# Halved first transfers, ScalarE diagonals and a re-ordered prologue in an attention and MLP kernel

## The chip, the cores and the metric

One core of a Trainium2 chip. The metric is device time in microseconds (us) of the whole program, the median of several runs. TensorE (PE, with its weight loads as PEld), VectorE (DVE), ScalarE (ACT) and GpSimd (POOL) each work through a list of instructions in order and wait for each other by semaphores; SyncE (SP) issues the transfers (DMAs) between the chip's main memory and SBUF.

## The reference, cut to what matters

```python
# r, k, v: (4, 8, 768, 48);  w, u: (8, 48)
for t in range(S):                       # S = 768
    cur = einsum('bhd,bhe->bhde', u * kt, vt)
    y[:, :, t] = einsum('bhd,bhde->bhe', rt, state + cur)
    state = w * state + einsum('bhd,bhe->bhde', kt, vt)
x = y.transpose(0, 2, 1, 3).reshape(B * S, H * D)      # 3072 x 384
h = x @ w_in                                          # 384 x 2048
g = 0.5 * h * (1 + erf(h / sqrt(2)))
out = g @ w_out                                       # 2048 x 384
```

## The kernel before, in words

The recurrence is done in chunks of 128 time steps (six chunks), each in four groups of two heads. For a group of the first chunk `first_group` (L525) does this: DVE multiplies keys and receptances `T` by powers of w into `Ts` (L535) and multiplies keys with receptances into `RK` (L541); PE sums `RK` with weights `u` (`sum_pairs`, L549); ACT copies the eight sums per row from PSUM to `cs` (L554); POOL spreads them over the diagonal of `Am` with one select over 128 x 1024 elements (`on_diagonal`, L496); PE makes the scores from `Ts` (L562); DVE copies their lower triangle over `Am` (L567, a predicated copy); PE multiplies `Am` by the values (L581); `keep` splits the result into a high and a low part, ACT for the high one (L509), DVE for the low one (L510). The score products of a group use the same PSUM bank as its sums, so they wait for the copy to `cs`.

The powers of w come first: a small transfer brings w and u (`wu_sb`, L357), DVE clamps w into `W` (L407), squares up to 64 powers (L412) and makes the inverses (L418, L419); ACT makes further powers (`state_powers`, L430 and L428) and copies them into `E` (L451).

The MLP runs in 96 steps: six chunks, 16 slices of 128 hidden units. A step has nine products for the first layer (`moe1`, L768), two Gelus on ACT (L800, L801), a difference on DVE (L802), and nine products for the second layer (`moe2`, L812). In the first 16 steps the weights of each slice must be split into two parts: a transfer of 768 KB (L464), three ACT operations (L479, L482, L488) and two DVE operations (L484, L491). Groups of later chunks (`prepare`, `products`, `state`) are put between the steps. PE is kept warm before the first step by products of zeros (L395) wherever the plan has a gap. At the end of a chunk the three banks `O` are scaled and stored; the last chunk's third bank is cut in two halves (`O[2]` and `Y`), each scaled by ACT (L851) or DVE (L848) and stored by SP (L854).

`count_plain` (L872) counts how many w lie in the range for which this form holds: DVE (L867 to L871), a product (L875), a copy to an integer (L877), and a load of it into a register of every engine (`values_load`, L878). After the last step all engines branch on it (L989).

The order on every engine is made by the class `Plan`: each operation is given an engine, a duration, a due time and the names it reads and writes; `play` simulates the engines and issues in order of simulated start, and a random search over due times with a fixed seed keeps the order whose simulated end is earliest. A change of any entry can therefore change the order everywhere. `port=True` marks operations of DVE and POOL that the plan doesn't let overlap; a POOL operation so marked gets a real wait on the last such DVE operation before it.

Of the kernel before, what the change touches and what calls it, by code (L numbers as in the profile page):

```python
# [24 lines left out]
C = 128  # L25
# [25 lines left out]
AT_LOADS, AT_E = 14000, 15000  # L51

SCALE = ("dd", "d", "d", "d")
PRODUCT = ("d", "d", "d", "d")

# [219 lines left out]
def rwkv_gelu_mlp(tc, rkT, rkv, wuT, uN, wmlp, r, k, vT, w, u, out):  # L275
    nc = tc.nc
    with ExitStack() as ctx:
# [63 lines left out]
        pool = lambda n: 200 + n * 2.1  # L341
        select_ns = lambda n: 100 + n * 8 * 1.5

# [26 lines left out]
        add("pool", 290, 4, lambda: select(ident, 0, -1, ALU.is_equal), r=["ones"], w=["ident"])  # L370

        for x in wa:
            add("pool", 750, 5, lambda x=x: nc.gpsimd.memset(x, 0), w=["wa"], port=False)

# [29 lines left out]

        def powers():
            nc.vector.memset(W[:, :, HALF:HALF + 1], 1.0)
            nc.vector.tensor_scalar(out=W[:, :, HALF + 1:HALF + 2], in0=w_sb.unsqueeze(2), scalar1=WMIN, scalar2=WMAX,  # L407
                                    op0=ALU.max, op1=ALU.min)
            n = 1
# [11 lines left out]

        add("dve", 1500, 5, powers, r=["w_sb"], w=["P"], port=True)
        add("dve", 520, 6, inverses, r=["P"], w=["Wi"], port=True)

# [17 lines left out]

        add("act", 1700, LATER, state_powers, r=["P"], w=["WKs"])
# [4 lines left out]
        add("pool", 320, 5, lambda: nc.gpsimd.memset(E[32:64, :, :, 1], 1.0), w=["E0"], port=False)  # L448
        for i, (src, dst, h) in enumerate(((slice(0, LP), slice(0, LP), 0), (slice(0, D), slice(64, LP), 1),
                                           (slice(64, LP), slice(0, D), 1))):  # L450
            add("act", act(512), AT_E, lambda src=src, dst=dst, h=h: nc.scalar.copy(  # L451
                out=E[dst].rearrange("l p a h i -> l (p a) h i")[:, :, h],
                in_=W[src].rearrange("l p (a i) -> l (p a) i", a=2)[:, :, 32:32 + HALF]),
                r=["Wi", "P", "WKs"], w=[f"E{(1, 2, 0)[i]}"], port=False)
# [66 lines left out]
        def first_group(gi, at, XX, XB, y, YB):  # L521
# [6 lines left out]
            sums, CS = cs[gi], f"cs{gi}"  # L528
            halves = SCALE[gi]
            for i, e in enumerate(halves):  # L530
                nb = NB // len(halves)
# [5 lines left out]
                        in1=W[:, p, 0:C].unsqueeze(1).unsqueeze(1).to_broadcast([LP, 2, nb, C]), op=ALU.mult),  # L537
                    r=["P", "Wi", f"T{gi}"], w=[f"{TR}{b}" for b in range(bs.start, bs.stop)], port=True)
            me = PRODUCT[gi]
            mul = nc.vector.tensor_tensor if me == "d" else nc.gpsimd.tensor_tensor  # L540
            add("dve" if me == "d" else "pool", dve(512) if me == "d" else pool(512), LATER, lambda: mul(  # L541
                out=RK[gi], in0=T[gi][:LP, 0, :, ::-1], in1=T[gi][:LP, 1], op=ALU.mult), r=[f"T{gi}"], w=[f"RK{gi}"], port=True)

            def sum_pairs():
                for b in range(NB):
                    for h in range(2):
# [268 lines left out]
        def moe2(m, at, dest):  # L815
# [3 lines left out]

            def go(m, n, which, at):  # L820
                j = m % NJ
                high, low, GH, GL = hidden(m)
                add("pe", MM * sum(parts[i][3] - parts[i][2] for i in which) / TOK, at, lambda: [product2(j, high, low, n, parts[i]) for i in which],
                    r=[f"{('wh', 'wl', 'wh')[n]}{2 * j + 1}", (GH, GH, GL)[n]], w=[banks[i] for i in which])

# [8 lines left out]
            elif m == NSTEP - 1:  # L834
                for q, i in ((1, 0), (1, 1), (5, 2), (4, 2), (0, 0), (0, 1), *((q, 2) for q in range(LEFT - 3, -1, -1)),
                             *((q, 3) for q in range(LEFT - 1, -1, -1))):
                    at += 2000
                    for n in range(3):
                        go(m - q, n, (i,), at + n)
            if j < NJ - 1:  # L840
                return
            last = m == NSTEP - 1
            for i, (d, bank, a, b) in enumerate(parts):
# [9 lines left out]
                if last:  # L853
                    dma(512 * (b - a), at + 2000, lambda d=d, a=a, b=b, o=o: nc.sync.dma_start(dest[d][:, a:b], o), r=[R])  # L854
            if not last:
                dma(128 * 6144, at + 20000, lambda: nc.sync.dma_start(
                    dest.rearrange("d p n -> p d n"), flat2(raw[0]).bitcast(F32).rearrange("p (d n) -> p d n", d=3)),
                    w=[f"raw0{i}" for i in range(3)])

# [12 lines left out]

        def count_plain(at):
# [76 lines left out]
        def swap():  # L950
# [7 lines left out]
        add("do", 0, SWAP_DUE, swap, w=["late", "ident", "ones", "diag", "past", "P", "WKs", "WN", "zeros", "warm", "spread"] +  # L958
            ["Wi"] + [f"{x}{i}" for x in ("T", "RK", "Nk", "Nv") for i in range(NP)] +
            [f"Ts{i}{b}" for i in range(NP) for b in range(NB)] + [f"Am{i}{j}" for i in (2, 3) for j in range(2)])  # L960
# [4 lines left out]
        for G in range(NSTEP + 1):  # L965
# [114 lines left out]
```

## Time and profile before

| | us |
|---|---|
| median of 3 runs (lowest, highest) | 449.92 (449.80, 450.51) |
| the profiled execution's own time | 449.15 |
| its span, first to last instruction | 447.0 |
| PE busy | 438.1 (98%) |
| DVE, ACT, POOL busy | 228.7, 178.7, 81.2 |
| granted TensorE clock, mean | 0.998 |

PE matmuls are pipelined and their ends modelled, so 98% is not PE at its peak; what matters is whether the next product could start. The profiled execution lies 2.15 us above its span and 0.77 us under the median of the runs.

### The profile page before, as it was taken

The numbers are of one execution on the slowest core, as the hardware profiler recorded it, in microseconds if no ns is written. First come the engines' busy times: TensorE is split into PE (matmuls) and PEld (weight loads), VectorE is DVE, ScalarE is ACT, GpSimd is POOL, SyncE is SP. The second block draws the span as 40 slices with busy tenths as digits, with TensorE's granted clock in tenths as the row PEclk, the third lists the DMA queues.
The fourth block names the chain that finished last, engine by engine and source line by source line (L and its number), as shares of the span: only waits on it lengthen the run. The fifth ranks groups of instructions, "written<-read, shape, count | busy, mean of one in ns | idle before, by whom it ended". The sixth has DMA issues, their size and how long they took to land.

```text
span 447.0 us, 10460 instructions
## 1 busy us (share of the span) xinstructions
PE 438.1 (98%) x4618; PEld 378.2 (85%) x4618; DVE 228.7 (51%) x342; ACT 178.7 (40%) x305; POOL 81.2 (18%) x98
## 2 busy tenths in 40 slices
PE   7999999999999999999999999999999999999995
PEld 5788888888888887888888888888888888888884
DVE  7989999975624367153546343544434311211111
ACT  7699998432322223232224222223322223322221
POOL 5533130324110222011211202202202000000000
PEclk9999999999999999999999999999999999999999
DMA  7986785223303034030333121313403000100002
GB/s 299 409 295 251 263 300 191 87 79 120 114 2 113 1 114 172 0 114 4 110 112 118 57 72 41 114 32 108 145 3 111 13 1 13 71 1 0 1 1 76
DMA packets 13570, 46.15 MB, mean 103 GB/s; under 512 B 1808, under 2 KB 2192, under 8 KB 13520
## 3 DMA queue, kind: packets, MB, share of 16 engines
q1 hardware_dynamic: 13520, 45.42, 29.7%
q8 instruction: 38, 0.62, 0.6%
q14 instruction: 12, 0.10, 0.1%
HBM read 38.73 MB, written 4.72 MB: 97 GB/s over the span
## 4 chain that ended last, share of the span: by engine, by line
PE 96%; DVE 1%; ACT 1%; DMA 0%; issue 0%; POOL 0%; DVEq 0%
PE Hp L768 42%; PE O L812 41%; PE Y L678 3%; PE A L686 2%; PE Y L706 2%; PE A L695 2%; PE Y L812 1%; PE O L581 1%; PE A L562 1%; PE O L768 1%; PE Y L562 0%; PE O L575 0%; ACT W L428 0%; PE A L603 0%; DMA wu_sb<-in_wuT_dram 0%; DVE W L412 0%
## 5 line engine op out<-in xcount | busy, mean ns | idle before, releaser
L768 PE MATMUL Hp<-xx,wh 128*128 128x512 f32 x570 | 156.3, 382 | 0.0
L800 ACT ACTIVATE gh<-Hp 128x512 fp32r<-128x512 f32 x91 | 54.3, 597 | 187.7 <-PE Hp L768 187.7
L802 DVE TENSOR_TENSOR gl<-gf,gh 128x512 fp32r<-128x512 f32 x92 | 65.7, 714 | 117.7 <-ACT gf L801 115.1
L768 PEld LDWEIGHTS Hp<-xx,wh 128*128 128x128 f32 x570 | 105.6, 189 | 15.4 <-issue 0.2
L768 PE MATMUL Hp<-xx,wl 128*128 128x512 f32 x285 | 77.4, 379 | 0.0
L812 PE MATMUL O<-gl,wh 128*128 128x512 f32 (+1 forms) x276 | 74.3, 376 | 0.8 <-DVE Sa L735 0.8
L812 PE MATMUL O<-gh,wl 128*128 128x512 f32 (+1 forms) x276 | 74.0, 375 | 0.0
L812 PE MATMUL O<-gh,wh 128*128 128x512 f32 (+1 forms) x276 | 73.9, 375 | 0.0
L768 PEld LDWEIGHTS Hp<-xx,wl 128*128 128x128 f32 x285 | 53.7, 189 | 7.7
L812 PEld LDWEIGHTS O<-gh,wh 128*128 128x128 f32 x276 | 52.0, 189 | 7.7 <-ACT gh L800 0.4
L801 ACT ACTIVATE gf<-Hp 128x512 f32<-128x512 f32 x95 | 56.3, 593 | 5.3 <-PE Hp L768 4.1
L812 PEld LDWEIGHTS O<-gl,wh 128*128 128x128 f32 x276 | 51.0, 189 | 8.3 <-issue 1.2
L812 PEld LDWEIGHTS O<-gh,wl 128*128 128x128 f32 x276 | 51.3, 189 | 6.8
L634 DVE TENSOR_TENSOR Tb<-Tb,E 112x1024 f32<-112x1024 f32 x20 | 26.5, 1325 | 31.4 <-DMA Tb<-in_rkT_dram 31.3
L637 POOL TENSOR_TENSOR Nb<-Nb 128x384 f32<-128x384 f32 x20 | 20.3, 1017 | 112.0 <-DMA Nb<-in_rkv_dram 48.8
L640 POOL TENSOR_TENSOR Nb<-Nb,WN 128x384 f32<-128x384 f32 x20 | 26.3, 1316 | 32.4 <-DVE Tb L634 19.4
L646 DVE TENSOR_REDUCE cs<-Nb 128x8 f32<-128x384 f32 x20 | 11.0, 552 | 24.1 <-POOL Nb L643 24.1
L735 DVE SCALAR_TENSOR_TENSOR Sb<-Sa,E,A 48x192 f32<-48x192 f32 x40 | 16.5, 413 | 11.2 <-PE A L695 10.5
L643 POOL TENSOR_TENSOR Nb<-Nb,u_sb 128x384 f32<-128x384 f32 x20 | 20.1, 1003 | 9.6 <-DVE gl L802 9.6
L509 ACT CAST xx<-Y 112x512 fp32r<-112x512 f32 x15 | 8.8, 585 | 31.7 <-PE Y L706 31.7
L716 POOL MEMSET done<- 1x1 f32 x19 | 1.7, 89 | 105.2 <-PE Y L678 105.2
L479 ACT ACTIVATE wa<-raw 128x768 f16<-128x768 bf16 x16 | 19.4, 1209 | 0.0
(128 smaller groups left out, 384.5 us busy)
## 6 DMA issues: line engine op xcount, KB each, us to landing
raw<-in_wmlp_dram SPq DMA_DIRECT2D x16, 767.8 KB, 5.6
Nb<-in_rkv_dram SPq DMA_DIRECT2D x20, 576.0 KB, 4.5
Tb<-in_rkT_dram SPq DMA_DIRECT2D x20, 512.0 KB, 6.0
out_dram<-raw SPq DMA_DIRECT2D x5, 768.0 KB, 3.7
T<-in_rkT_dram SPq DMA_DIRECT2D x4, 512.0 KB, 5.2
xx<-x SPq DMA_DIRECT2D x30, 64.0 KB, 4.4
N<-in_rkv_dram SPq DMA_DIRECT2D x4, 384.0 KB, 10.0
out_dram<-raw SPq DMA_DIRECT2D x2, 256.0 KB, 4.1
```

Of the source, the lines that this page charges most:

```text
L479: add("act", 930 if j < 2 else 1110, LATER, lambda: nc.scalar.activation(out=a.bitcast(F16).rearrange("p (n t) -> p n t", t=2)[:, :, 1], i ...
L634: add("dve", 1140, LATER, lambda: nc.vector.tensor_tensor(out=flat, in0=flat, in1=E[:, p, 0].rearrange("l h i -> l (h i)").unsqueeze(1).to ...
L637: add("pool", pool(DM), LATER, lambda: nc.gpsimd.tensor_tensor(out=n[:, 0], in0=n[:, 0], in1=n[:, 1], op=ALU.mult), r=[NK], w=[NR])
L640: add("pool", pool(DM), LATER, lambda: nc.gpsimd.tensor_tensor(out=kn, in0=kn, in1=WN2[:, p].rearrange("s j d -> s (j d)").unsqueeze(1).to ...
L643: add("pool", pool(DM), LATER, lambda: nc.gpsimd.tensor_tensor(out=n[:, 0], in0=n[:, 0], in1=u_sb[:, p, :].unsqueeze(1).to_broadcast([C, N ...
L678: last[:] = [nc.tensor.matmul(YU[quarter(j), h, b * HALF:(b + 1) * HALF], lhsT=S2[h][l, b, :], rhs=t[l, 0, b, times(h)], start=(b == 0), s ...
L735: add("dve", 430, at, lambda l=l, x=x: nc.vector.scalar_tensor_tensor(out=out[quarter(1 - x)], in0=src[l], scalar=E[l, p, 1, h, 32:33], in ...
L768: nc.tensor.matmul(dst, lhsT=wt[j][:, 0, k_ * 128:(k_ + 1) * 128], rhs=pairs(x[:, a, k_, :]), start=start and k_ == ks[0], stop=stop and k ...
L800: add("act", 480, LATER, lambda: nc.scalar.activation(out=high, in_=dst, func=AF.Gelu, scale=256.0), r=[H_], w=[GH])
L801: add("act", 480, LATER, lambda: nc.scalar.activation(out=gf, in_=dst, func=AF.Gelu, scale=256.0), r=[H_], w=["gf"])
L802: add("dve", dve(512), LATER, lambda: nc.vector.tensor_tensor(out=low, in0=gf, in1=high.bitcast(F32), op=ALU.subtract), r=["gf", GH], w=[G ...
L812: nc.tensor.matmul(dst[:, a:b], lhsT=wt[j][:, 1, d * 128:(d + 1) * 128], rhs=pairs(gt)[:, a // 2:b // 2], start=(j == 0 and n == 0), stop= ...
```

## The change

1. `T[0]` comes in two transfers (batches 0 and 1, then 2 and 3); the product `RK[0]` and its sums on PE are done by the same halves. Other groups keep one transfer, one product, one set of sums.
2. The diagonals of groups 0 and 2 are no longer made by a POOL select but by eight ACT operations of 128 x 128 each (a copy of `diag` scaled by one column of the sums). Groups 1 and 3 keep the select, now with `port=True`, and with 1.08 us in the plan where it had 1.64 us.
3. The clamp of w is an operation of its own, due before all else on DVE. The second `memset` of `wa` on POOL and the `memset` of `E` now wait for it; the first doesn't.
4. Durations in the plan: inverses 520 to 560 ns, state powers 1700 to 2080, copies to `E` 487 to 630, the `memset` of `E` 320 to 520.
5. `count_plain` moves from step 32 to step 38, its DVE part now behind that step's low Gelu part, and the register load is an entry of 620 ns on DVE instead of 0 ns on no engine.
6. In the last steps the products into `Y` (the fourth part) are ordered behind those into `O[2]`.
7. The store of the third piece of the last chunk is issued by ACT instead of SP. The stores of the five other chunks are each cut in two transfers (two thirds and one third).

```diff
-            dma(C * 4096, at, lambda: nc.sync.dma_start(T[s], rkT[gi]), r=r, w=[f"T{s}"])
+            for bs in (slice(0, 2), slice(2, 4)) if gi == 0 else (slice(0, NB),):
+                dma(C * 1024 * (bs.stop - bs.start), at, lambda bs=bs: nc.sync.dma_start(
+                    T[s][:, :, bs], rkT[gi][:, :, bs]), r=r, w=...)
...
+        add("dve", 170, -10 ** 6, clamp, r=["w_sb"], w=["P0"], port=True)
+        for n, x in enumerate(wa):
+            add("pool", 750, 5, lambda x=x: nc.gpsimd.memset(x, 0), r=["P0"] * n, w=["wa"], port=False)
+        add("dve", 1380, 5, powers, r=["P0"], w=["P"], port=True)
...
-            add("pe", 650, LATER, sum_pairs, r=[f"RK{gi}", "w_sb"], w=XB)
+            for bs in parts:
+                nb = bs.stop - bs.start
+                add("dve", dve(128 * nb), LATER, lambda bs=bs: nc.vector.tensor_tensor(
+                    out=RK[gi][:, bs], in0=T[gi][:LP, 0, bs, ::-1], in1=T[gi][:LP, 1, bs], op=ALU.mult),
+                    r=TN(bs), w=[f"RK{gi}{bs.start}"], port=True)
+                add("pe", 220 + 110 * nb, LATER, lambda bs=bs: sum_pairs(bs), r=[f"RK{gi}{bs.start}", "w_sb"], w=XB)
...
-            add("pool", select_ns(C), LATER, lambda: on_diagonal(am, C, sums), r=[CS], w=[f"{AM}0", f"{AM}1"], port=False)
+            if OWN[gi] == "s":                                   # OWN = "asas"
+                add("pool", select_ns(C), LATER, lambda: on_diagonal(am, C, sums), r=[CS], w=[f"{AM}0", f"{AM}1"], port=True)
+            else:
+                for n in range(2 * NB):
+                    j, b = divmod(n, NB)
+                    add("act", 185 + C / 1.2, LATER, lambda n=n, j=j, b=b: nc.scalar.activation(
+                        out=am[:, j, b, :], in_=diag, func=AF.Copy, scale=sums[:, n:n + 1]), r=["diag", CS], w=[f"{AM}{j}"])
...
+                if last and i == 2:
+                    add("act", 400, at + 1000 + i, lambda d=d, a=a, b=b, o=o: nc.scalar.dma_start(dest[d][:, a:b], o), r=[R])
...
-            add("dve", 800, at, in_range, r=["w_sb", "xx00h"], w=["n1"])
+            add("dve", 800, at, in_range, r=["w_sb", behind], w=["n1"])
...
-            add("do", 0, at, lambda: plain.append(nc.values_load(n2, min_val=0, max_val=LP * NP)), r=["n2"])
+            add("dve", 620, at, lambda: plain.append(nc.values_load(n2, min_val=0, max_val=LP * NP)), r=["n2"])
...
-            if G == 2 * NJ:
-                count_plain(step_at(G))
+            if G == 2 * NJ + 6:
+                count_plain(step_at(G), hidden(G)[3])
```

## Rows read from the trace of the kernel before

**Rows 1.** Busy time by stage (stretch: length, busy us of each engine, clock, DMA)

```profile
5.25:15.39 10.14, 8.82 (x174) 6.65 (x175) 9.15 (x13) 7.43 (x19) 4.39 (x3) 1.00 1.01 399
15.39:22.76 7.37, 7.37 (x134) 5.54 (x134) 7.37 (x8) 5.40 (x8) 4.82 (x4) 1.00 1.02 397
34.00:50.00 16.00, 16.00 (x194) 13.77 (x193) 15.79 (x23) 16.00 (x20) 3.08 (x4) 1.00 0.75 266
85.00:441.90 356.90, 355.93 (x3551) 310.28 (x3541) 148.59 (x232) 105.80 (x194) 51.63 (x63) 1.00 0.20 65
```

**Rows 2.** Chain of work that ended last: one undisturbed run of nine products

```profile
45.07 1.94 PE Hp L768 x9
```

**Rows 3.** Timeline of PE, then DVE, around the count at 169 us (start, us, instruction)

```profile
168.68 0.81 PE L812 MATMUL O<-gh,wh 128*128 128x512 f32 x3
169.55 0.09 PEld L875 LDWEIGHTS A<-n 112*1 112x1 f32 x2 [0.47 <-DVE Sb L735]
...
170.66 0.15 DVE L877 CAST n<-A 1x1 int32<-1x1 f32 x1
...
171.35 0.51 PEld L812 LDWEIGHTS O<-gl,wh 128*128 128x128 f32 x3 [1.17 <-issue]
...
172.11 0.81 PE L768 MATMUL Hp<-xx,wh 128*128 128x512 f32 x3
```

**Rows 4.** Tile n: the register load (ns min/median/max, first and last start)

```profile
L878 PEldq TENSOR_LOAD <-n x1: 485/485/485, 170.8 to 170.8; - x1
```

**Rows 5.** Line 854's instructions, then the timeline of the last stores

```profile
L854 SPq DMA_DIRECT2D out_dram<-raw x3: 343/382/2007, 439.8 to 440.7; - x3
...
439.78 2.92 SPq L854 DMA_DIRECT2D out_dram<-raw  x3
439.93 0.39 ACT L851 ACTIVATE raw<-O 128x256 f32<-128x256 f32 x1 [0.17 <-PE O L812]
441.94 0.42 DVE L848 TENSOR_SCALAR Nb<-Y 128x256 f32<-128x256 f32 x1 [1.87 <-PE Y L812]
442.80 0.37 SPq L854 DMA_DIRECT2D out_dram<-Nb  x1
```

**Rows 6.** The clamp and its neighbours at the start, and line 867, its like

```profile
2.43 0.79 DVE L407 TENSOR_SCALAR W<-wu_sb 112x4 f32<-112x4 f32 x1 [0.91 <-DMA wu_sb<-in_wuT_dram]
2.46 0.74 POOL L373 MEMSET wa<- 128x768 int32 x1
...
L867 DVE TENSOR_SCALAR low<-wu_sb x1: 159/159/159, 116.1 to 116.1; 112x4 f32<-112x4 f32 x1
```

**Rows 7.** Timeline of DVE and POOL around the first diagonals

```profile
5.25 0.69 DVE L541 TENSOR_TENSOR RK<-T 112x512 f32<-112x512 f32 x1
8.41 3.18 POOL L496 TENSOR_SCALAR_AFFINE_SELECT Am<-cs 128x1024 f32<-128x1024 f32 x2 [4.63 <-ACT cs L554]
10.46 1.30 DVE L567 COPY_PREDICATED Am<-past,A 128x1024 f32<-128x1024 uint32 x1 [0.99 <-POOL Am L496]
```

**Rows 8.** Timeline of ACT: what stands after each of its idle times

```profile
12.92 0.17 ACT L554 COPY cs<-A 128x8 f32<-128x8 f32 x1 [2.49 <-PE A L549]
12.98 1.09 ACT L479 ACTIVATE wa<-raw 128x768 f16<-128x768 bf16 x1
16.07 0.17 ACT L554 COPY cs<-Y 128x8 f32<-128x8 f32 x1 [0.76 <-PE Y L549]
20.48 0.59 ACT L509 CAST xx<-O 128x512 fp32r<-128x512 f32 x1 [1.30 <-PE O L581]
25.23 0.48 ACT L607 COPY Sa<-A 112x384 f32<-112x384 f32 x1 [1.03 <-PE A L603]
```

**Rows 9.** ACT line 428 by shape, 0 to 40 us (us busy, mean ns), then its merged timeline row

```profile
L428 ACT ACTIVATE W<-W 112x64 f32<-112x64 f32 x4 | 1.1, 335 | 0.0
L428 ACT ACTIVATE W<-W 112x32 f32<-112x32 f32 x4 | 0.9, 304 | 0.0
...
4.90 1.91 ACT L428 ACTIVATE W<-W 112x64 f32<-112x64 f32 x8
```

**Rows 10.** Transfers issued at 1.29 and at 3.87 us (count, KB, us to landing)

```profile
T<-in_rkT_dram SPq DMA_DIRECT2D x1, 512.0 KB, 3.4
...
raw<-in_wmlp_dram SPq DMA_DIRECT2D x1, 767.8 KB, 8.6
```

**Rows 11.** Timeline, DVE and PE: the weights of the fifth slice and their first use

```profile
39.03 1.69 DVE L491 TENSOR_TENSOR wl<-wb,wh 128x768 fp32r<-128x768 f32 x1
40.90 0.81 PE L768 MATMUL Hp<-xx,wl 128*128 128x512 f32 x3
```

More of the change, by code (lines that the diff above doesn't have):

```diff
@@ L51 @@
 AT_LOADS, AT_E = 14000, 15000
+OWN = "asas"
 SCALE = ("dd", "d", "d", "d")
-PRODUCT = ("d", "d", "d", "d")
 class Plan:
@@ L350, in load_group @@
             s = slot(gi)
-            dma(C * 4096, at, lambda: nc.sync.dma_start(T[s], rkT[gi]), r=r, w=[f"T{s}"])
+            for bs in (slice(0, 2), slice(2, 4)) if gi == 0 else (slice(0, NB),):
+                dma(C * 1024 * (bs.stop - bs.start), at, lambda bs=bs: nc.sync.dma_start(
+                    T[s][:, :, bs], rkT[gi][:, :, bs]), r=r, w=[f"T{s}{b}" for b in range(bs.start, bs.stop)] if gi == 0 else [f"T{s}"])
             if gi < NP:
@@ L370, in rwkv_gelu_mlp @@
         add("pool", 290, 4, lambda: select(ident, 0, -1, ALU.is_equal), r=["ones"], w=["ident"])
-        for x in wa:
-            add("pool", 750, 5, lambda x=x: nc.gpsimd.memset(x, 0), w=["wa"], port=False)
         for dst, src, x in ((diag2, diag, "diag"), (past2, past, "past")):
@@ L402, in rwkv_gelu_mlp, with clamp @@
         plan.heat_from = add("pe", 430 * HEATS, 10, warm_up, r=["zeros"], w=["H", "A0", "A1", "O0", "O1", "O2", "Y", "U"])
-        def powers():
+        def clamp():
             nc.vector.memset(W[:, :, HALF:HALF + 1], 1.0)
@@ L408, in powers @@
                                     op0=ALU.max, op1=ALU.min)
+        def powers():
             n = 1
@@ L420, in inverses @@
                                            op=ALU.mult)
-        add("dve", 1500, 5, powers, r=["w_sb"], w=["P"], port=True)
-        add("dve", 520, 6, inverses, r=["P"], w=["Wi"], port=True)
+        add("dve", 170, -10 ** 6, clamp, r=["w_sb"], w=["P0"], port=True)
+        for n, x in enumerate(wa):
+            add("pool", 750, 5, lambda x=x: nc.gpsimd.memset(x, 0), r=["P0"] * n, w=["wa"], port=False)
+        add("dve", 1380, 5, powers, r=["P0"], w=["P"], port=True)
+        add("dve", 560, 6, inverses, r=["P"], w=["Wi"], port=True)
         def state_powers():
@@ L529, in first_group @@
             halves = SCALE[gi]
+            parts = (slice(0, 2), slice(2, 4)) if gi == 0 else (slice(0, NB),)
+            TN = lambda bs: [f"T{gi}{b}" for b in range(bs.start, bs.stop)] if gi == 0 else [f"T{gi}"]
             for i, e in enumerate(halves):
@@ L537, in first_group, with sum_pairs @@
                         in1=W[:, p, 0:C].unsqueeze(1).unsqueeze(1).to_broadcast([LP, 2, nb, C]), op=ALU.mult),
[L538 to L545, printed above, removed]
+                    r=["P", "Wi", *TN(bs)], w=[f"{TR}{b}" for b in range(bs.start, bs.stop)], port=True)
+            def sum_pairs(bs):
+                for b in range(NB)[bs]:
                     for h in range(2):
@@ L818, in moe2, with go @@
             banks = ["O0", "O1", "O2", "Y"][:len(parts)]
-            def go(m, n, which, at):
+            def go(m, n, which, at, behind=()):
                 j = m % NJ
@@ L823, in go @@
                 add("pe", MM * sum(parts[i][3] - parts[i][2] for i in which) / TOK, at, lambda: [product2(j, high, low, n, parts[i]) for i in which],
-                    r=[f"{('wh', 'wl', 'wh')[n]}{2 * j + 1}", (GH, GH, GL)[n]], w=[banks[i] for i in which])
+                    r=[f"{('wh', 'wl', 'wh')[n]}{2 * j + 1}", (GH, GH, GL)[n], *behind], w=[banks[i] for i in which])
             if m == 0:
@@ L852, in moe2 @@
                         out=o, in_=bank[:, a:b], mul=256.0), r=[banks[i]], w=[f"{R}{'' if last else i}"])
-                if last:
+                if last and i == 2:
+                    add("act", 400, at + 1000 + i, lambda d=d, a=a, b=b, o=o: nc.scalar.dma_start(dest[d][:, a:b], o), r=[R])
+                elif last:
                     dma(512 * (b - a), at + 2000, lambda d=d, a=a, b=b, o=o: nc.sync.dma_start(dest[d][:, a:b], o), r=[R])
             if not last:
-                dma(128 * 6144, at + 20000, lambda: nc.sync.dma_start(
-                    dest.rearrange("d p n -> p d n"), flat2(raw[0]).bitcast(F32).rearrange("p (d n) -> p d n", d=3)),
-                    w=[f"raw0{i}" for i in range(3)])
+                for some in (slice(0, 2), slice(2, 3)):
+                    dma(128 * 2048 * (some.stop - some.start), at + 20000, lambda some=some: nc.sync.dma_start(
+                        dest[some].rearrange("d p n -> p d n"),
+                        flat2(raw[0]).bitcast(F32).rearrange("p (d n) -> p d n", d=3)[:, some]),
+                        w=[f"raw0{i}" for i in range(some.start, some.stop)])
         low = sb([LP, NP], F32, "low")
@@ L958, in rwkv_gelu_mlp @@
         add("do", 0, SWAP_DUE, swap, w=["late", "ident", "ones", "diag", "past", "P", "WKs", "WN", "zeros", "warm", "spread"] +
-            ["Wi"] + [f"{x}{i}" for x in ("T", "RK", "Nk", "Nv") for i in range(NP)] +
+            ["Wi"] + [f"{x}{i}" for x in ("T", "Nk", "Nv") for i in range(NP)] +
+            [f"T0{b}" for b in range(NB)] + ["RK02"] + [f"RK{i}0" for i in range(NP)] +
             [f"Ts{i}{b}" for i in range(NP) for b in range(NB)] + [f"Am{i}{j}" for i in (2, 3) for j in range(2)])
```

12 lines of the change are left out of this document (6 added, 6 removed).

## The prediction, on record before the changed kernel ran

> **What bounds the kernel now.** I read the busy time by stage first, then the chain of work that ended last, then the waits and the timeline where PE stood. From 22.8 us, the first MLP product, to 441.9 us PE is the bound: between 85 and 441.9 us it lacks 0.97 of 356.90 us, while DVE and ACT are busy 42% and 30% of that time [rows 1]. What is removed there counts only if it is PE time, and nearly the only idle PE time is at the count at 169 us [rows 3]. So three places can move the end: the front (until PE has real work without a break), the count, and the tail behind the last product.
>
> In the front no single engine is the bound. From 5.25 to 15.39 us DVE works 9.15 of 10.14 us, the missing 0.99 being one wait for the POOL select [rows 1, 7]. The transfer engines are full to 1.0 until 22.8 us [rows 1]: the first weights' transfer, issued at 3.87 us, needs 8.6 us and lands at 12.5, and the first ACT operation on it starts at 12.98 [rows 8, 10]. From 34 to 50 us ACT is busy 16.00 of 16.00 us and DVE 15.79 [rows 1]. PE never stands there either, but the weights come just in time: the low part of the fifth slice's is done at 39.03 + 1.69 = 40.72 us and its first product starts at 40.90 [rows 11]. So to gain, PE, DVE and ACT must all be earlier; an engine that comes later than now stops PE a fraction of a microsecond on.
>
> **The change part by part.** All sums are made against the profiled execution, 449.15 us with a span of 447.0.
>
> The count. From 168.68 to 172.11 us, 3.43 us, PE does nine products of the second layer and the two small ones of the count; nine products undisturbed take 1.94 [rows 2, 3]. The count costs 3.43 - 1.94 = 1.49 us. It consists of a wait of 0.47 for a state update on DVE that still used the bank, and of 1.17 before the next weight load: until the integer is there (170.66 + 0.15 = 170.81) and then a register load of 0.485 [rows 3, 4]; products already handed to the array cover the rest. Step 38 lies between two groups of the later chunks (these come every fourth step: 36, 40), so no state update holds the bank, and the integer's copy finds DVE mostly idle. The wait of 0.47 and the delay before 170.81 go. What remains is the register load, on PE's sequencer too. If the two or three products ahead of it hide it, the count costs about 0.2 and the gain is 1.3. If the new wait on the low Gelu part makes the count late against the plan, PE stands about as long as now for n1 and again for the load, 0.47 + 0.485 and the small products, and the gain is 0.3. Queued behind that wait on DVE are the next step's difference and a group's work; DVE is idle more than half of that stage. I take 1.0, that is a load half hidden: the nearest row has the load itself exposed, but at the end of 1.17 us that had emptied the array.
>
> The tail. SP needs 0.34 and 0.38 us to issue the first two output pieces and 2.01 for the third; it is free at 439.78 + 2.92 = 442.70 and issues the last piece at 442.80, though DVE had that ready at 441.94 + 0.42 = 442.36 [rows 5]. With the third on ACT, which has nothing after its copy ends at 440.32 [rows 5], SP can issue the last at 442.38: 0.42 less. If the transfer also has the engines to itself it lands a little sooner, which I bound by another 0.3; if SP's hold comes from the first two transfers being in flight and not from the third instruction, the last piece is held in its place and the gain is 0. I take 0.4, as the row shows the last piece's issue short once the third was through. The Trainium skill (DMA: Bandwidth & Descriptors, section Issuing engines are not separate DMA queues) says that transfers from several engines run on the same 16 DMA engines and that issuing on several saves only the sequencer's issue time, usually small. By that rule the gain would be just the issue time; here one issue took 2.01 us, so rule and row part on its size. Ordering the `Y` products behind `O[2]` changes nothing: in this trace they are already in that order, and PE has no gap there. Cutting the chunk stores adds five issues of about 0.4 us on SP, which is idle for tens of microseconds then; 0.
>
> The front, head of DVE. The clamp takes 0.79 us on 112 x 4 elements; an operation of the same shape takes 0.16 later; it ran beside the second `memset` of `wa` on POOL [rows 6]. With that `memset` behind it, 0.79 - 0.16 = 0.63 us go, and powers, inverses and ACT's state powers all start that much earlier. That puts DVE at 4.62 us where it now starts on `T[0]` at 5.25 [rows 7]; `T[0]` whole lands at 1.29 + 3.4 = 4.69 [rows 10], so its first half arrives in time and the halving is what lets DVE use the 0.63. It costs one more small issue on SP and one more fixed part on DVE (0.06). The moved `memset`s run beside the powers; POOL has no work until 8.41 [rows 7], so they have room. Should the stretched clamp have another reason (the end is then 0), the halving has nothing to win. The Trainium skill (SBUF — State Buffer, section Who interferes with whom) says that VectorE in a two-port mode and GpSimd block each other for a whole instruction, whoever starts first. By that rule the 0.63 is all gain.
>
> The front, the wait for the select: with the first diagonal on ACT, the predicated copy at 10.46 no longer waits 0.99 for POOL [rows 7]. So DVE could be 0.63 + 0.99 = 1.62 us earlier at the top.
>
> The front, ACT. Sixteen copies are added. A scaled copy of 32 columns takes 304 ns and one of 64 takes 335, eight follow each other in 1.91 us, 0.24 each [rows 9]; 128 columns add 2 x 31 ns to 64, so 0.30 each at most and 16 x 0.29 = 4.6 us. ACT's idle time between 10 and 26 us is 2.49 + 0.76 + 1.30 + 1.03 = 5.58 [rows 8], and the head gives 0.63 more. If all of it could be filled, ACT would come out 1.6 us ahead. But the weights' transfers set when the splits start: the first can come forward by 12.98 - 12.5 = 0.5 at most, and the second set of eight falls among the splits of the first two slices, with idle of only 0.76 and 1.30 about it. So the front's gain lies between 1.6 us (all of DVE's lead reaches PE) and minus 2.3 (one whole set of eight, 8 x 0.29, is added to the chain of the weights). POOL's selects that stay now wait for DVE's products; behind them on POOL wait only the keys' products for the states, which aren't urgent. I take 0.3 gained: the weights' arrival allows 0.5, and an order with some idle time keeps part of that.
>
> Sum: 1.0 + 0.4 + 0.3 = 1.7 us. Span 447.0 - 1.7 = 445.3, its execution 447.45, and against the median 449.92 - 1.7 = 448.2 us. The plan's search runs anew, so all orders differ. After 85 us there is only 0.97 us of idle to lose, so a new order can hardly win there, but it can lose: I allow 0.5, the size of the single wait at the count.
>
> **The rivals.**
> A. All of DVE's lead reaches PE: 1.62 in front, with 1.4 at count and tail: 449.92 - 3.0 = 446.9. For it: DVE is the busiest engine from 5.25 to 22.76 us. Against: ACT full, weights landing at 12.5.
> B. ACT becomes the bound of the first steps, slower than before: the second set of eight copies is put ahead of the weight splits, which then reach PE 2.3 us later for good, as ACT is full from 34 to 50 us and can't catch up. With count and tail at 0.8 and 0.4: 449.92 + 2.3 - 1.2 = 451.0. It decides the sign once ACT's first splits come more than about 1.5 us later than now. For it: 16.00 of 16.00 us; the margin of 0.18 us at the fifth slice. Against: 5.58 us of idle earlier.
> C. The change doesn't do what it says: the count only moves its stall (0.3), the last store is held in SP in place of the third (0), and ACT's copies eat DVE's lead: 449.6.
>
> **How the numbers follow.** The forecast, 448.2 with its own range 447.3 to 449.1, has 0.44; A 0.17; B 0.20; C 0.19. A measurement of this kernel can tell about 0.2%, 0.9 us, from no change: faster is below 449.0, slower above 450.8. Faster: nearly all of the forecast's 0.44 and A, 0.60. Same: C and the near part of B, with the forecast's upper end, 0.25. Slower: 0.15. The range takes in A at its lower end, less 0.2, and reaches up to B's middle: 446.7 to 450.8.
>
> **What would show it.** Clamp of about 0.16 us and `RK` before 4.9 us: head right. No wait of the first predicated copy for its diagonal: right on the select. ACT's first weight split before 12.98 and the eighth slice's products no later than before, relative to the first MLP product: ACT has absorbed the copies; if PE waits for `wl` or `wh` between 25 and 55 us, B. First MLP product: before 22.76 us. Around the count nine products within 2.2 to 2.5 us instead of 3.43. The last store issued within 0.1 us of DVE's copy. I am wrong if the first product comes earlier and PE then waits for weights, or if a wait appears in the middle, where today there is none.

## The result, and the profile after

The changed kernel takes 451.97 us (450.00 to 454.33, twelve executions), the kernel before in the same comparison 449.68 (448.78 to 450.75): a ratio of 1.0051, 95% interval 1.0036 to 1.0066. So it is 0.5% slower, and that is clear of noise. The profiled execution of after took 450.0 us, with a span of 447.8 us. It is the shortest of the twelve, so its rows show what costs time even in a short execution, and not what makes the longer ones long.

The clamp, the products of keys with receptances and two predicated copies, from the timeline of DVE (start, us, instruction, idle time before it and what ended it), kernel after:

```profile
2.60 0.63 DVE L406 TENSOR_SCALAR W<-wu_sb 112x4 f32<-112x4 f32 x1 [1.07 <-DMA wu_sb<-in_wuT_dram]
...
5.26 0.42 DVE L557 TENSOR_TENSOR RK<-T 112x256 f32<-112x256 f32 x1
...
6.08 0.42 DVE L557 TENSOR_TENSOR RK<-T 112x256 f32<-112x256 f32 x1 [0.40 <-DMA T<-in_rkT_dram]
...
8.34 0.69 DVE L557 TENSOR_TENSOR RK<-T 112x512 f32<-112x512 f32 x1 [0.64 <-DMA T<-in_rkT_dram]
...
11.82 1.33 DVE L580 COPY_PREDICATED Am<-past,A 128x1024 f32<-128x1024 uint32 x1
...
18.64 1.33 DVE L580 COPY_PREDICATED Am<-past,A 128x1024 f32<-128x1024 uint32 x1 [0.95 <-ACT Am L569]
```

Against [rows 6, 7]: the clamp is still stretched, 0.63 us in place of 0.79; `RK` starts at the same 5.26; two waits for `T` have appeared (0.40 and 0.64), and the first predicated copy has lost its wait for the select but starts at 11.82 instead of 10.46. The other copy, of group 2, now waits 0.95 for its diagonal from ACT. SP's four issues of `T` take it to 3.74, and the first product of the MLP comes at 24.54, where it came at 22.76. Timeline of SP, then of PE, after:

```profile
1.28 2.46 SPq L352 DMA_DIRECT2D T<-in_rkT_dram  x4
```

```profile
24.54 0.48 PE L781 MATMUL Hp<-xx,wh 128*128 128x512 f32 x1
```

Two parts went as wished. The count, timeline of PE and DVE, after (compare [rows 3]):

```profile
198.59 0.81 PE L781 MATMUL Hp<-xx,wh 128*128 128x512 f32 x3
...
199.34 0.19 PE L892 MATMUL A<-n 112*1 112x1 f32 x2
...
199.46 0.92 PE L781 MATMUL Hp<-xx,wl 128*128 128x512 f32 x3
...
199.56 0.41 DVE L748 SCALAR_TENSOR_TENSOR Sa<-Sb,E,A 48x192 f32<-48x192 f32 x1 [0.20 <-PE A L892]
199.98 0.14 DVE L894 CAST n<-A 1x1 int32<-1x1 f32 x1
...
200.21 0.59 PE L781 MATMUL Hp<-xx,wh 128*128 128x512 f32 x2
```

From the first to the third group of three products it is 200.21 - 198.59 = 1.62 us; undisturbed it would be 6/9 of 1.94, 1.29 [rows 2]. So the count costs 0.33 where it cost 1.49: 1.2 us gained. State updates on DVE (L748) stand beside it here too, one of them right ahead of the integer's copy. The last stores, timeline of SP, ACT's queue and DVE, after (compare [rows 5]):

```profile
441.21 0.81 SPq L869 DMA_DIRECT2D out_dram<-raw  x2
...
441.78 0.39 ACTq L867 DMA_DIRECT2D out_dram<-raw  x1
...
443.37 0.42 DVE L861 TENSOR_SCALAR Nb<-Y 128x256 f32<-128x256 f32 x1 [1.87 <-PE Y L825]
...
443.86 0.33 SPq L869 DMA_DIRECT2D out_dram<-Nb  x1
```

No issue takes 2.0 us any more, and the last store is issued 0.07 us behind DVE's copy instead of 0.44.

And a wait has come where there was none: the waits of PE between 25 and 440 us (waited for; us in total, times, longest), after:

```profile
PE A L708 <- POOL done L729: 1.2, 1, 1.2
```

It stands at 73 us. The timeline of POOL, then of DVE, beside it:

```profile
71.16 3.05 POOL L653 TENSOR_TENSOR Nb<-Nb,WN 128x384 f32<-128x384 f32 x1 [5.45 <-DVE gl L815]
```

```profile
70.92 0.97 DVE L488 CUSTOM_DVE_ANT_0 wb<-wb,wa 128x1536 uint16<-128x1536 uint16 x1
71.79 0.97 DVE L495 TENSOR_TENSOR wl<-wb,wh 128x768 fp32r<-128x768 f32 x1
72.66 0.70 DVE L815 TENSOR_TENSOR gl<-gf,gh 128x512 fp32r<-128x512 f32 x1
```

A POOL product whose like takes 1.0 us takes 3.05; it ends 0.9 us after the third of three DVE operations in a row. PE's products L708 read what it writes (`Nb`), and the small `done` memset named by the view is merely the last thing queued on POOL.

### The profile page after: what moved, and what is told of

It reads as the page before. It is cut to its first block, busy times and chain, and to the rows that moved or that the text cites. A ratio compares the mean times of both kernels' runs of the same rounds, so it can differ in the third digit from the quotient of the medians.

```text
span 447.8 us, 10490 instructions
## 1 busy us (share of the span) xinstructions
PE 439.8 (98%) x4622; PEld 379.6 (85%) x4622; DVE 226.1 (50%) x343; ACT 184.1 (41%) x321; POOL 77.8 (17%) x96
## 4 chain that ended last, share of the span: by engine, by line
PE 90%; DVE 4%; DMA 1%; ACT 1%; issue 1%; POOL 1%; SPq 0%; POOLq 0%
PE Hp L781 39%; PE O L825 38%; PE Y L691 2%; PE Y L719 2%; PE A L699 2%; PE A L708 2%; DMA T<-in_rkT_dram 1%; PE Y L825 1%; PE O L594 1%; DVE wl L495 1%; DVE wb L488 1%; DVE gl L815 1%; POOL Nb L653 1%; DVE Tb L647 1%; PE Hp L394 0%
## 5 line engine op out<-in xcount | busy, mean ns | idle before, releaser
L815 DVE TENSOR_TENSOR gl<-gf,gh 128x512 fp32r<-128x512 f32 x92 | 64.7, 703 | 119.5 <-ACT gf L814 115.9
L748 DVE SCALAR_TENSOR_TENSOR Sb<-Sa,E,A 48x192 f32<-48x192 f32 x40 | 16.5, 413 | 11.1 <-PE A L708 10.4
```

What stands on the lines that cost most here:

```text
L748: add("dve", 430, at, lambda l=l, x=x: nc.vector.scalar_tensor_tensor(out=out[quarter(1 - x)], in0=src[l], scalar=E[l, p, 1, h, 32:33], in ...
L815: add("dve", dve(512), LATER, lambda: nc.vector.tensor_tensor(out=low, in0=gf, in1=high.bitcast(F32), op=ALU.subtract), r=["gf", GH], w=[G ...
```

## The experiments

My theories, as the result was seen: P, `T[0]` in two transfers makes `T` late; Q, ACT's sixteen copies hold up the weights; R, the new order, with POOL beside DVE, loses elsewhere. A fourth, W, came out of the later runs. Unless said otherwise each kernel keeps the order of all instructions on every engine, so that only the edited thing differs.

**`T[0]` whole, in the changed kernel.**

```
-  T[s][:, :, 0:2], then T[s][:, :, 2:4]      # two dma_start
+  T[s]                                       # one
```

> The changed kernel with its order kept on every engine; the one difference: the first keys and receptances come in one transfer of 512 KB (rows of 4 KB) where it had two of 256 KB (rows of 1 KB twice), and nothing is issued in the place of the second. Theory P (the halved transfer makes all that follows it land later; VectorE waited 0.40 us for the second half and 0.64 us for the next group): both waits go, the first MLP product comes about 1 us before 24.5 us, and the ratio to the kernel before falls from 1.005 to about 1.003. Theory Q (the sixteen copies on ScalarE hold up the weights) and theory R (the new order loses, by waits between GpSimd and VectorE later on): the ratio stays at 1.005.

Measured: 449.12 us (448.02 to 451.21), ratio 0.9984 (0.9967 to 1.0001). Timeline of DVE, then PE's first MLP product:

```profile
5.35 0.76 DVE L557 TENSOR_TENSOR RK<-T 112x256 f32<-112x256 f32 x2
...
7.23 0.69 DVE L557 TENSOR_TENSOR RK<-T 112x512 f32<-112x512 f32 x1
...
10.70 1.32 DVE L580 COPY_PREDICATED Am<-past,A 128x1024 f32<-128x1024 uint32 x1
...
17.65 1.32 DVE L580 COPY_PREDICATED Am<-past,A 128x1024 f32<-128x1024 uint32 x1 [1.08 <-ACT Am L569]
```

```profile
23.54 0.48 PE L781 MATMUL Hp<-xx,wh 128*128 128x512 f32 x1
```

The waits for `T` are gone, the first product is 1.0 us earlier than after's, and the median 2.85 us lower. P holds: the second transfer costs nearly three times the 1.0 that the profiled execution of after shows. This is still 0.78 us later than before's 22.76.

**All four diagonals by select.**

```
-  eight nc.scalar.activation(out=am[:, j, b, :], in_=diag, scale=sums[:, n:n + 1])
+  on_diagonal(am, C, sums)                   # POOL, also for groups 0 and 2
```

> The changed kernel with its order kept; the one difference: the diagonals of groups 0 and 2 are made by the GpSimd select as before, in the places of the first of the eight copies, and ScalarE has none of the sixteen copies (4.6 us less work). Theory Q: ScalarE splits the second and third slice's weights 2 us sooner, the first MLP product comes 1 to 2 us sooner, ratio 1.000 to 1.003. Theories P and R: no gain beyond 0.3 us, ratio 1.004 to 1.006.

> The kernel after with T[0] in one transfer and all four diagonals by POOL selects, none by ScalarE; orders kept. Theory Q (the 16 ScalarE copies hold up the weight splits): faster than with T[0] whole alone (ratio 0.9984 to before), 448.0 to 448.6 us. Without Q (they fit into ScalarE's idle time, and save DVE's wait for the select): the same or slower, 449.1 to 450.1 us.

Measured: with the two transfers 453.33 (450.58 to 455.25), ratio 1.0069 (1.0042 to 1.0097); with `T[0]` whole 450.48 (450.02 to 451.60), ratio 1.0014 (1.0005 to 1.0024). By the medians ACT's copies are worth 1.4 us each time (453.33 - 451.97, 450.48 - 449.12). With `T[0]` whole the two intervals don't overlap; with the two transfers they do (1.0042 to 1.0097 against 1.0036 to 1.0066), so there it isn't shown. Q, by which the kernel would have become faster, falls.

**The memset really waiting for the clamp.** In the changed kernel the wait of the second `memset` of `wa` stands in the plan alone; here it is a wait of the instruction.

```
+  after(second_memset, clamp)
```

> The changed kernel with its order kept; the one difference: the second memset of wa on GpSimd now really waits for the clamp on VectorE (in the changed kernel the plan puts it behind the clamp but no wait holds it, and it started at 2.47 us, before the clamp at 2.60). If the memset is what stretches the clamp: 0.63 us become about 0.16 us and VectorE reaches the first product of keys and receptances at about 4.8 instead of 5.26 us. Theory P: VectorE then waits longer for the second half, and the time gains less than 0.2 us. If the stretch has another cause, the clamp stays at 0.6 us.

> The kernel after with its order kept, T[0] in one transfer and the second memset of wa really waiting for the clamp. Theory P (what the change lost, it lost by the halved transfer): with T[0] whole at 4.7 to 5.0 us and a clamp of 0.17 us, RK[0] starts at 5.0 in place of 5.35, the first MLP product 0.3 us earlier than with T[0] whole alone (23.54), 448.6 to 449.0 us. Theory R (the new order and POOL beside DVE cost as much as they win): no earlier first product, 449.0 to 449.6 us.

Measured: 451.84 (450.59 to 454.99), ratio 1.0045 (1.0015 to 1.0075); with `T[0]` whole too, 449.55 (449.29 to 450.60), ratio 0.9996 (0.9986 to 1.0005). Timeline of DVE in the latter:

```profile
2.65 0.17 DVE L406 TENSOR_SCALAR W<-wu_sb 112x4 f32<-112x4 f32 x1 [1.12 <-DMA wu_sb<-in_wuT_dram]
...
5.09 0.76 DVE L564 TENSOR_TENSOR RK<-T 112x256 f32<-112x256 f32 x2 [0.16 <-DMA T<-in_rkT_dram]
...
18.00 1.33 DVE L587 COPY_PREDICATED Am<-past,A 128x1024 f32<-128x1024 uint32 x1 [1.62 <-ACT Am L576]
```

The memset is what stretches the clamp: 0.17 us without it. But the lead isn't passed on: `RK` then waits for `T[0]`, and at 18.0 DVE waits 1.62 for ACT's diagonal where it waited 1.08. Neither pair of medians shows a gain.

**The halving alone, in the kernel before.**

```
-  nc.sync.dma_start(T[s], rkT[gi])
+  the same in two, for gi == 0: [:, :, 0:2] and [:, :, 2:4]
```

> The kernel before with its order kept; the one difference: the first keys and receptances come in two transfers of 256 KB (rows of 1 KB twice), issued one after the other. Theory P: the first group lands 1.3 us later than at 4.7 us, the second about 2 us later, VectorE waits for both, and the time rises by about 1 us, ratio 1.002. Theories Q and R: ratio within 0.001 of 1.

Measured: 453.90 (450.44 to 456.68), ratio 1.0082 (1.0049 to 1.0116). This one edit costs 4 us and spreads the executions over 6 us, where the kernel before spreads over 2.

**Is it the shorter pieces or the second transfer?** Cutting the last axis makes pieces of 1 KB out of rows of 4 KB. Apart: one transfer walked in pieces of 1 KB; two transfers (partitions 0 to 63, 64 to 127) of 4 KB pieces.

```
+  "p a (h b) t -> p (a h) (b t)" [:, ::-1]   # on both sides, one dma_start
```

```
+  T[s][0:64], then T[s][64:128]              # two dma_start
```

> The kernel before with its order kept on every engine; only the transfer of T[0] is changed: still one instruction for all 512 KB, but walked in pieces of 1 KB (each row of 4 KB as four pieces, last one first). Theory S (the size of the pieces makes the halved load slow): as slow as with two transfers in the kernel before, 452 to 454 us and a wide spread, RK[0] not before 5.8 us and a wait of RK[1] for its transfer of about 1 us. Theory N (the second transfer as such makes it slow, by what it puts in front of T[1]): 449.5 to 450.2 us, RK[0] at 5.2 to 5.5, no wait of RK[1] over 0.3 us.

> The kernel before with its order kept; T[0] in two transfers by partitions, 0 to 63 and 64 to 127, so that every piece stays 4 KB long. Theory S: 449.5 to 450.5 us, as before, with RK[0] later by no more than SP's extra issue of 0.6 us. Theory N: 452 to 454 us, RK[0] after 6 us and a wait of RK[1] of about 1 us.

Measured: 451.09 (449.60 to 456.15; three of nine above 455), ratio 1.0068 (1.0030 to 1.0105), and 454.33 (450.87 to 456.40), ratio 1.0089 (1.0053 to 1.0124). `RK` began at 5.79 and 6.20 us, after waits of 0.45 and 0.86. Neither theory alone: each way makes `T[0]` late. (In neither trace does DVE wait for `T[1]`; with two transfers of 1 KB pieces it waits 1.22 us.) The traced execution of the first is only 0.5 us late there, and yet three of its nine last some 6 us longer than the kernel before. That disproportion was the new question, and the second kernel's profile, taken from an execution of 455.85 us, points at an answer. Timeline of PE:

```profile
4.72 1.05 PE L396 MATMUL A<-zeros 128*128 128x512 f32 x2
5.57 0.63 PE L396 MATMUL Y<-zeros 128*128 128x512 f32 x1
6.95 1.10 PE L550 MATMUL A<-wu_sb,RK 48*64 48x48 f32 x32 [0.75 <-DVE RK L542]
...
13.44 2.08 PE L563 MATMUL Y<-Ts 64*128 64x128 f32 x16
...
19.08 2.05 PE L563 MATMUL A<-Ts 64*128 64x128 f32 x16
21.06 0.50 PE L396 MATMUL Hp<-zeros 128*128 128x512 f32 x1
21.49 0.68 PE L550 MATMUL Y<-wu_sb,RK 48*64 48x48 f32 x32
...
23.78 1.16 PE L563 MATMUL Y<-Ts 64*128 64x128 f32 x16
```

The products of zeros at the start follow each other at 0.43 us for 512 columns, which is the 1.2 GHz level. PE then stood 0.75 us, and until about 21 us the same 16 score products took 2.05 to 2.08 us that take 1.16 afterwards, at 2.4 GHz. (The PEclk line of the profile's page gives full speed here; the level is read from the products' lengths.) Theory W: a late `T` leaves PE without work while its clock is at the lower level or has just risen, and then the clock comes back only near 20 us.

**Three more warm-up products, on that kernel.**

```
-  for n in range(HEATS):
+  for n in range(HEATS + 3):
```

> The kernel before with T[0] in two transfers by partitions (4 KB pieces) and three more warm-up products of zeros, 13 in place of 10, so that PE has work until about 7.1 us; all orders kept. Without the three more, this kernel took 454.33 us (450.87 to 456.40), and in the traced execution PE stood 0.75 us before the first sums at 6.95, stayed at products spaced 0.43 us (the 1.2 GHz level) and did 16 score products in 2.08 us instead of 1.16 until about 20 us. Theory W (the late transfer costs mainly because PE stands in front of the sums while its clock is still at the lower level, and in part of the executions the clock then rises only near 20 us): no execution over 453.5, median 450.3 to 452.0, and the 16 score products at 1.16 us. Theory P (the time lost is the later arrival of T itself): 454 us as without them.

Measured: 451.51 (450.62 to 452.06), ratio 1.0027 (1.0016 to 1.0039). Timeline of PE:

```profile
6.42 0.79 PE L396 MATMUL O<-zeros 128*128 128x512 f32 x2
7.14 0.68 PE L550 MATMUL A<-wu_sb,RK 48*64 48x48 f32 x32
```

W: 2.8 of the 4.6 us are gone and no execution is above 452.1, though `T[0]` is no earlier (`RK` at 6.25). The rest, 1.6 us, is left to P. Part of it is that DVE, now later, meets POOL's selects: the operation into `Ts` at 8.66 takes 2.11 us, where the kernel before has 1.22.

**Three warm-up products fewer, in the kernel before.** Its transfers are untouched.

```
+  for n in range(HEATS - 3):
```

> The kernel before with three warm-up products fewer, 7 in place of 10; transfers and all orders as before, so PE has no work from about 4.7 us until the first sums at 6.0. Theory W: part of the executions at 454 to 457 us, median above 451, a spread of several us; if the traced execution is one of these, score products of 2.1 us per 16 until about 20 us. Theory P: 449.5 to 450.2 us with a spread under 2 us, since T comes as early as before.

Measured: 455.15 (454.34 to 457.07), ratio 1.0128 (1.0105 to 1.0151). Timeline of PE:

```profile
3.43 1.48 PE L395 MATMUL O<-zeros 128*128 128x512 f32 x3
5.99 0.68 PE L549 MATMUL A<-wu_sb,RK 48*64 48x48 f32 x32 [1.07 <-DVE RK L541]
...
8.32 0.72 PE L562 MATMUL A<-Ts 64*128 64x128 f32 x8 [0.86 <-ACT cs L554]
8.96 1.11 PE L549 MATMUL Y<-wu_sb,RK 48*64 48x48 f32 x32
...
11.88 2.08 PE L562 MATMUL Y<-Ts 64*128 64x128 f32 x16
...
19.83 0.68 PE L549 MATMUL Y<-wu_sb,RK 48*64 48x48 f32 x32
```

Here the clock had risen by 5.99, PE stood 1.07 and again 0.86 us, and the clock fell at about 8.9 and came back shortly before 19.4 (products at 1.2 GHz, then at 2.4). In the kernel before, the same two places, with products of zeros ahead of the first:

```profile
5.99 0.68 PE L549 MATMUL A<-wu_sb,RK 48*64 48x48 f32 x32 [0.45 <-DVE RK L541]
...
8.32 0.72 PE L562 MATMUL A<-Ts 64*128 64x128 f32 x8 [0.87 <-ACT cs L554]
8.97 0.68 PE L549 MATMUL Y<-wu_sb,RK 48*64 48x48 f32 x32
```

The gaps are 0.45 and 0.87 us there, and the clock stays. 0.6 us more of idle time, with every transfer as before, costs 5.2 us in the median of four executions. W is shown in these two kernels. But a gap doesn't bring the clock down in every execution. The traced execution of the halving alone, 451.91 us long, has larger ones, and the sums behind them still take 0.68 us, which is the 2.4 GHz level. Timeline of PE:

```profile
7.12 0.68 PE L550 MATMUL A<-wu_sb,RK 48*64 48x48 f32 x32 [1.30 <-DVE RK L542]
...
10.24 0.68 PE L550 MATMUL Y<-wu_sb,RK 48*64 48x48 f32 x32 [1.01 <-DVE RK L542]
```

What its rows show lost is the late `T`, for which DVE waits 1.03 and then 1.22 us: the first MLP product comes at 24.76, 2.0 us later than in the kernel before. What decides whether the clock falls stays open.

**The same fillers in the changed kernel.** First two more products ahead of the first sums, then three there and three ahead of the second group's sums.

```
+  for n in range(HEATS + 2):
```

```
+  for n in range(HEATS + 3):
+  for n in range(3): heat(Hp)                # in sum_pairs, if gi == 1
```

> The kernel after with two more warm-up products, 12 in place of 10, PE busy until about 6.7 us instead of 6.0; orders kept. Theory W: the spread of 450.0 to 454.3 shrinks to within about 450 to 452 and the median goes from 452.0 to 450.3 to 451.2. Theory P: 451.7 to 452.7 with the same spread.

> The kernel after, T[0] in two transfers as it is, with three more warm-up products ahead of the first sums and three ahead of the sums of the second group, so that PE doesn't stand in either place. Orders kept. Theory W (the slow executions of after are those whose clock rose late because PE stood): no execution over 452.5, median 450.5 to 451.3. Theory P (the second transfer's own delay of T[0] and T[1], which differs between executions): the spread of 450 to 454 and a median of 451.7 to 452.7 stay.

Measured: 451.94 (450.45 to 453.16), ratio 1.0052 (1.0035 to 1.0068): the median stays, the highest of four executions is 1.2 us lower than after's, no clear verdict; W's median was missed. Then 451.19 (449.72 to 451.81), ratio 1.0030 (1.0016 to 1.0044): nothing above 451.8, where after had six of its twelve executions at 452.2 and more. W had said so, and P that the spread would stay. In the changed kernel, then, the longest executions fit W, about 0.8 us of the median; it is not shown, as the intervals overlap and no long execution of this kernel was traced. The other 2.1 us down to `T[0]` whole are P; the traced execution still has DVE waiting 2.21 us for `T[1]`. Timeline of DVE:

```profile
9.48 0.69 DVE L560 TENSOR_TENSOR RK<-T 112x512 f32<-112x512 f32 x1 [2.21 <-DMA T<-in_rkT_dram]
```

How late `T[1]` comes differs from one execution to the next: in the traces with two transfers of 1 KB pieces DVE waits between 0.55 and 2.21 us for `T[1]`, and in those with `T[0]` whole not at all.

**The tail alone, in the kernel before.**

```
-  nc.sync.dma_start(dest[d][:, a:b], o)
+  (nc.scalar if i == 2 else nc.sync).dma_start(dest[d][:, a:b], o)
```

> The kernel before with its order kept, only the store of the third piece of the last chunk issued by ScalarE. By my sum for the tail: 0.4 us less, 449.3 to 449.4 us, the last store issued within 0.15 us of DVE's copy and last product to end of span 4.7 to 5.0 us in place of 5.4. If the long issue comes from the stores ahead and not from the third, the last store is held on SP for some 2 us and the time stays at 449.7.

Measured: 449.61 (448.87 to 450.36), ratio 0.9992 (0.9982 to 1.0002): between 0.8 gained and 0.1 lost. The last store is issued at 442.64, 0.06 behind DVE's copy, so SP's hold is gone, but from the last product's start to the end of the span it took 5.7 us, not 4.7 to 5.0: the transfer itself landed later in this execution. Over all traces that stretch is 4.5 to 5.7 us with the store on ACT (twelve traces, mean 5.2) and 5.2 to 5.8 without (six, mean 5.4).

**The product that PE waits for at 73 us.** With `T[0]` whole, that POOL product once without its wait for the DVE operation ahead of it (a wait that only keeps the engines apart), once on DVE.

```
-  elif held is not None and issue:
+  elif held is not None and issue and n not in self.alone:     # alone: L653 of group 7
```

```
-  nc.gpsimd.tensor_tensor(out=kn, in0=kn, in1=WN2[:, p] ...)
+  (nc.vector if gi == 7 else nc.gpsimd).tensor_tensor(...)
```

> The kernel after with T[0] in one transfer, and one POOL product (keys of the later group 7 by powers, 3.05 us at 70.0 us) without its wait for the VectorE operation before it; that wait keeps the two engines apart and carries no data. Orders kept. Theory V (the 1.2 us for which PE stands at 72 us come from this product, which is released at 70.0 and then blocked by three VectorE operations in a row): it starts at 64.6, is done before 71, and the time is 1.2 us under that of T[0] whole alone, 447.8 to 448.3 us. If every VectorE operation blocks it, it is done no earlier than now and the time stays at 449.1.

> The kernel after with T[0] in one transfer and that same product done by VectorE (about 0.5 us) in its place in the order. Theory V: PE stands for at most 0.2 us at 72 us, 447.9 to 448.5 us. If something else of the same group comes late too (its scores, its receptances), the wait stays near 1 us and the time at 448.9 to 449.3.

Measured: 448.56 (448.28 to 448.78), ratio 0.9969 (0.9957 to 0.9982), and 448.24 (447.80 to 448.93), ratio 0.9963 (0.9951 to 0.9976). Without the wait, timeline of POOL and the waits of PE:

```profile
64.57 1.71 POOL L654 TENSOR_TENSOR Nb<-Nb,WN 128x384 f32<-128x384 f32 x1
```

```profile
PE O L828 <- DVE gl L818: 0.9, 1, 0.9
```

It ran 5.5 us earlier in 1.71 us, but PE now waits 0.9 for a low Gelu part, and the median missed the 447.8 to 448.3 expected. With the product on DVE no wait is left; busy time from 50 to 85 us (PE first):

```profile
50.00:85.00 35.00, 34.97 (x436) 29.91 (x438) 33.61 (x46) 30.78 (x40) 6.37 (x8) 1.00 0.58 186
```

PE has 34.97 of 35.00 us, where with `T[0]` whole alone it has 33.75. Its median is the lowest of all, 0.9 us under `T[0]` whole alone, though the two intervals still touch; its profiled span is 445.6 us, 1.4 under before's.

**A new search with `T[0]` whole.**

```
-  for bs in (slice(0, 2), slice(2, 4)) if gi == 0 else (slice(0, NB),):
+  for bs in (slice(0, NB),):                 # in load_group; all orders found anew
```

> The kernel after with T[0] in one transfer, known to the plan, so that the search for the order runs anew. Theory R (what the changed front wins or loses behind 22 us is luck of the order): anything from 447.8, when no wait like the 1.2 us at 72 us is in it, to 450.0. With no part for the order it gives 449.1, as with the order kept.

Measured: 448.87 (448.00 to 450.02), ratio 0.9976 (0.9966 to 0.9987). Other orders, with one wait of 0.4 us left in place of 1.2, and a first product at 23.95 instead of 23.54. The interval overlaps that of `T[0]` whole with its order kept (0.9967 to 1.0001), so the new search is not shown to win or lose anything. For R there is only the wait at 73 us and what its removal gave, about 1 us.

## Why the prediction was wrong

I said 448.2, at most 450.8, and a gain; it was 451.97, and a loss. By its own steps:

- *"It costs one more small issue on SP and one more fixed part on DVE."* This step failed, and with it the sign. I gave a second transfer the price of its issue. It has two others. First, `T` comes later: DVE waits 0.40 for the second half and 0.64 for `T[1]`, which is worth 1.0 us in the shortest execution and about 2.1 us of the median. Second, it can leave PE standing among its first products of real data: 0.43 us ahead of the second group's sums in after's profile, 0.96 and 1.80 there in the two variants with the memset's wait and with four selects. In the kernel before, with three warm-up products fewer, more idle time of PE alone cost 5.2 us, the clock being at 1.2 GHz from about 9 to 19 us; in the changed kernel this fits the longest executions and isn't shown. I had [rows 3] for the wait at 169 us but asked of no wait ahead of the first MLP product what it does to the clock.
- *"With that memset behind it, 0.63 us go."* False twice. The entry orders the plan, not the instruction, so the memset still ran beside the clamp: I had read one line of the diff as a wait, and item 3 of the change, as I wrote it, holds of the plan alone. And where it does wait, the 0.46 us gained on the clamp end in waits for `T[0]` and for ACT. The reason for the stretch was right (0.63 to 0.17 us); by the Trainium skill's rule (SBUF — State Buffer, section Who interferes with whom) that is what a blocked port looks like, and the trace agrees, at 73 us as well (3.05 us for a product of 1.0).
- *Select's wait.* The 0.99 of the first predicated copy is gone as said, yet a like one (1.08 with `T[0]` whole) stands at group 2's, for ACT. I had named this place, the second set of eight, but as a cost for the weights. With `T[0]` whole the front loses 0.78 us where I had 0.3 gained; the range of 1.6 to minus 2.3 held it.
- *Rival B* came out near the measured time for the wrong reason. ACT is not the bound: from 34 to 50 us it is busy 15.76 of 16.00 us, less than before [rows 1], PE waits for no weights by more than 0.2 us, and taking ACT's copies away makes it slower. Rival A never began: the first MLP product came later in every version. C was right only in that ACT's copies eat DVE's lead, at group 2's diagonal.
- *The count*: 1.2 gained, 1.0 said; the register load is hidden altogether. My reason for step 38 was wrong, as state updates stand beside the count there too; what hides the load is the products ahead of it. That rests on the trace of after; no run had the count alone.
- *The tail*: 0.4 said. In the trace of after the end follows the last product's start by 4.7 us instead of 5.4 (443.06 to 447.8, 441.63 to 447.0), 0.6 gained; by the means over all traces it is about 0.3. Alone it measured 0.36 with an interval of -0.1 to 0.8. That SP's hold goes is shown, a gain in time isn't. The Trainium skill's rule that I weighed (DMA: Bandwidth & Descriptors, section Issuing engines are not separate DMA queues) would give the issue time and no more, which that interval allows, as it allows nothing at all; the long issue itself was 2.0 us on SP and 0.39 on ACT.
- *"I allow 0.5"* for a new order: the wait at 73 us is 1.2, and it hit a stretch that I had taken as safe because PE stood nowhere in it before. Removing it gives 0.9 us by the medians.

Together, in the profiled executions: first product 1.78 later, wait 1.2, count and tail 1.2 and 0.6 earlier; 1.2 us longer by this sum and 0.8 by the spans, the difference lying in small idle times not followed up. The forecast of 448.2 is met by the change with `T[0]` in one transfer and one product moved, 448.24, but that is chance: the first product still comes at 23.61 there, 0.85 us later than before, where I had 0.3 gained in front.

## What to carry to other kernels

Cutting a transfer in two isn't free because its second issue is short: look at what is queued behind it, and at who stands idle until it lands. In the first microseconds ask of every wait of PE what it does to the clock, for here a gap half a microsecond longer cost several, and filler products that reach to the real work are cheap. Where the executions spread widely, explain a long one and not the shortest, and see that a dependency in a plan is also a wait in the list of instructions.

## What the hardware showed that I had not expected

- After a gap of 0.75 us at about 6 us, or gaps of 1.07 and 0.86 up to 8.3 us, PE was at the 1.2 GHz level until about 21 and 19 us, although it then ran short products (weights of 64 x 128 or 48 x 64) almost without a break; after gaps of 1.30 and 1.01 us in another execution it stayed at 2.4 GHz. When the clock first rises differs between executions of nearly the same start: PE's products speed up at about 4.6 us with `T[0]` whole, at about 7.1 in after's profile, so that the same first sums are 0.78 us long in the one and 1.11 in the other (the two rows below). The Trainium skill (TensorE: Matmul & The Clock Gate, section What's actually happening) says that the lower level is the default, that activity releases it, and that the moment isn't tied to the kernel's start. The traces agree on the first and the last; on the second only for the first rise, as in the two executions named first PE worked almost without a break from 7 to 21 and from 9 to 19 us at 1.2 GHz.
- A POOL product of 1.0 us took 3.05 beside three DVE operations in a row, and 1.71 at another place in the order: how long POOL is held up differs with what DVE does then.
- With 512 KB in pieces of 1 KB, or as two transfers of 64 partitions each, the first product that needs them started 0.5 and 1.0 us later than with one transfer in pieces of 4 KB (5.79 and 6.20 against 5.25, one trace each).

PE's first sums, with `T[0]` whole and then in after's profile:

```profile
5.83 0.78 PE L551 MATMUL A<-wu_sb,RK 48*64 48x48 f32 x32 [0.37 <-DVE RK L557]
```

```profile
6.13 1.11 PE L551 MATMUL A<-wu_sb,RK 48*64 48x48 f32 x32
```
